# Seven query chunks in place of six in the first layer of a two-layer attention and gMLP kernel

## The chip, the cores and the metric

The kernel runs on one core of one Trainium2 chip. The metric is the device time of one execution in microseconds (us). A single execution of one kernel varies by up to 9 us in what follows, so times are medians of several runs, and the experiments below also use the clock that TensorE was granted in each run.

## The reference, cut to what matters

```python
def reference(A_x, A_wq, A_wk, A_wv, A_wo, B_x, B_w_in, B_w_sp, B_b_sp, B_w_out):
    x = A_x                                        # (1, 2048, 512), bf16
    x = x + _A_ref(_layernorm(x), ...)             # attention: 32 heads of 16, one K and V for all
    x = x + _B_ref(_layernorm(x), ...)             # gMLP: gelu, spatial 2048x2048 product, gate
    x = x + _A_ref(_layernorm(x), ...)             # the second layer, with the same weights
    x = x + _B_ref(_layernorm(x), ...)
    return x
```

The exps of the attention are the bulk: 2 layers x 32 heads x 2048 x 2048. The kernel works in blocks of 128 keys x 512 columns (queries times heads); there are 4096 of them.

## The kernel before

The kernel is a program that writes a program. It declares operations with dependences, an estimated duration and a priority. A greedy list scheduler inside it plays the five engines forward in time on those estimates, and at each step commits the operation that can start next. What it commits is written out as fixed instruction streams with semaphores. So the order of all instructions is settled before anything runs, and it depends on every estimate. `layer` is 0 for the first and 1 for the second layer; the lists below have one entry for each.

```python
self.chunks = [[512, 512, 512, 256, 128, 128]] * 2          # queries per chunk, for each layer
self.passes = [[(0, 8, 1), (8, 12, 2), (12, 15, 4)]] * 2    # spatial passes: key tiles s0:s1, after which chunk
self.gelus = [[(0, 1), (2,), (3, 4), (5,)]] * 2             # chunks whose GELUs are done together
...
def d_psum(n):                       # the estimates: VectorE on PSUM, ScalarE
    return n * 1.042e-3 + 0.066
def d_act(n):
    return n * 0.8333e-3 + 0.051
...
def make_q(self, q, war=()):         # the query projection of one set: n queries x 512/n slices of heads
    ...
    pairs = range(g.t0 // 256, (g.t0 + n - 1) // 256 + 1)
    pe_last, (op,) = sc.job([...], [...],
        [x for p in pairs for x in self.xnTA_ev[(g.layer, p)]] + self.c_wq[...], pr)
```

A query set of a chunk of 512 needs the transposed normalised X of four tiles (pairs 0 and 1); one of a chunk of 256 needs two tiles (pair 0). No score of a layer can be computed before its first query set is there. Each block of scores then gets its exp either on ScalarE (three or two blocks in one activation) or on VectorE (a chain of six instructions, two blocks at a time); the scheduler decides block by block. When a chunk's last group of heads is done, the chunk's output projection, layer norm and input product of the gMLP follow, among the exps of the next chunk. At the end of a layer comes the closing: the last spatial part, the gate, the output product, and, in the first layer, the keys of the second.

The softmax here doesn't subtract the row's maximum and nothing guards it: scores larger than these inputs give would overflow.

## Time and profile before

| | before |
|---|---|
| time, median of 3 runs | 1813.9 us (1811.8 to 1814.6) |
| span of the profiled run | 1813.8 us |
| ScalarE / VectorE busy | 96% / 95% |
| exp blocks on VectorE / on ScalarE | 532 / 3564 |

From the page of the kernel before. The first line is busy time, share of the span and number of instructions of each engine. The others are groups of instructions: line, engine, operation, tiles, shapes, count, then total busy us, mean ns of one, and the idle time before them.

```profile
PE 1579.3 (87%) x11647; PEld 463.8 (26%) x11730; DVE 1720.7 (95%) x2962; ACT 1732.7 (96%) x1561; POOL 48.5 (3%) x90
...
L1434 ACT ACTIVATE Pa<-ps_all 128x1024 bf16<-128x1024 f32 (+1 forms) x1430 | 1619.8, 1377 | 19.3 <-PE ps_all L1774 17.4
...
L1626 DVE TENSOR_SCALAR E<-ps_all 128x512 f32<-128x512 f32 x532 | 362.1, 684 | 23.3 <-PE ps_all L1774 20.5
L1755 PE MATMUL ps_all<-zero 128*128 128x512 bf16 x1066 | 326.8, 392 | 15.6 <-ACT z1s L1047 3.1
...
L1657 DVE SCALAR_TENSOR_TENSOR Pd<-E 128x1024 uint16<-128x1024 f32 x267 | 324.2, 1214 | 4.3
...
L1653 DVE TENSOR_TENSOR E<-E 128x1024 f16<-128x1024 f16 x267 | 182.7, 684 | 4.7
...
L1655 DVE TENSOR_TENSOR E<-E 128x1024 f16<-128x1024 f16 x267 | 182.3, 683 | 3.6
L1651 DVE TENSOR_SCALAR E<-E 128x1024 f16<-128x1024 uint16 x267 | 182.3, 683 | 1.6
...
L1654 DVE TENSOR_SCALAR E<-E 128x1024 f16<-128x1024 f16 x267 | 111.6, 418 | 2.1
```

TensorE (PE) has room: 327 us of its time are filler matmuls on a zero tile, which only keep it busy. ScalarE (ACT) and VectorE (DVE) are both full. The two are within a per cent of each other (96% and 95%).

The timeline of ScalarE of the kernel before: start us, us, engine, line, operation, tiles, shapes, count, and in brackets the idle time before it with what ended it.

```profile
9.24 0.98 ACT L725 ACTIVATE kT<-ps_all,mask 128x256 bf16<-128x256 f32 x2 [1.00 <-PE ps_all L703]
...
12.87 1.02 ACT L681 ACTIVATE xnTA<-ps_all 128x1024 bf16<-128x1024 bf16 x1 [0.93 <-PE ps_all L673]
...
14.21 0.59 ACT L828 ACTIVATE qs<-ps_all 128x512 bf16<-128x512 f32 x1
...
15.79 1.45 ACT L1434 ACTIVATE Pa<-ps_all 128x1536 bf16<-128x1536 f32 x1
```

The keys of pair 0 (kT) are copied by 10.2 us, but the queries (qs) only by 14.8 us, since they wait for pair 1; the first exp of the kernel starts at 15.79 us. ScalarE does not stand idle until then: between 12.87 and 15.79 us it does other copies (kT, V and xnTA, the transposed X), with one gap of 0.19 us. The next two lines are from the same engine's timeline at the boundary between the layers, where the exps of the first layer have ended (the table load follows the last one) and those of the second begin. The last line is from VectorE's timeline: the eviction of the first group of heads, a good mark of progress, as there are 64 of them.

```profile
864.86 1.28 ACT L1451 ACT_TABLE_LOAD   x1
...
900.72 1.45 ACT L1434 ACTIVATE Pa<-ps_all 128x1536 bf16<-128x1536 f32 x1 [1.25 <-PE ps_all L1774]
```

```profile
48.70 0.68 DVE L841 CAST oT<-ps_all 128x512 bf16<-128x512 f32 x1
```

### The profile page before, as it was taken

How to read it: one execution, taken by the hardware profiler on the slowest of the kernel's cores; microseconds unless marked ns; L12 is line 12 of the kernel's file. 1: busy time of each engine (PE TensorE's matmuls, PEld its weight loads, DVE VectorE, ACT ScalarE, POOL GpSimd, SP SyncE). 2: the span in 40 equal slices, each digit the busy share in tenths (PEclk: the TensorE clock that was granted, in tenths of full speed). 3: DMA queues.
4: the chain of work that ended last, by engine and by line, in shares of the span. 5: the costliest groups of instructions: out<-in, count | busy, mean ns of one | idle time of the engine just before them, and what ended most of it. 6: DMA issues, size and time to landing. Idle time of an engine off the chain costs nothing.

```text
span 1813.8 us, 29897 instructions
## 1 busy us (share of the span) xinstructions
PE 1579.3 (87%) x11647; PEld 463.8 (26%) x11730; DVE 1720.7 (95%) x2962; ACT 1732.7 (96%) x1561; POOL 48.5 (3%) x90
## 2 busy tenths in 40 slices
PE   8888888888889998898998888888888899989988
PEld 3222222222222222222432222222222222222334
DVE  8999999999999999987999999999999999999888
ACT  7999999999999999999589999999999999999983
POOL 2000000000000000000110000000000000000000
PEclk9999999999999999999999999999999999999999
DMA  5344110010010121121210001000110111212213
GB/s 158 100 113 103 35 27 7 7 30 18 16 47 28 29 53 47 36 59 57 52 44 7 7 7 19 18 7 4 30 24 13 44 30 30 47 28 52 65 57 113
DMA packets 154517, 75.65 MB, mean 42 GB/s; under 512 B 108548, under 2 KB 150792, under 8 KB 154376
## 3 DMA queue, kind: packets, MB, share of 16 engines
q1 hardware_dynamic: 152792, 73.56, 15.7%
q8 instruction: 94, 1.54, 0.4%
q14 instruction: 47, 0.39, 0.1%
q10 hardware_dynamic: 1584, 0.16, 0.1%
HBM read 30.97 MB, written 17.83 MB: 27 GB/s over the span
## 4 chain that ended last, share of the span: by engine, by line
ACT 43%; DVE 23%; issue 17%; PE 16%; DMA 1%; POOL 0%; ACTq 0%; POOLq 0%
ACT Pa L1434 41%; PE ps_all L1774 5%; DVE E L1626 3%; PE ps_all L1517 3%; PE ps_all L1158 3%; DVE Pd L1657 3%; DVE E L1653 2%; DVE st L641 2%; DVE E L1651 2%; DVE E L1655 2%; PE ps_all L1250 2%; PE ps_all L1755 1%; DVE gp L1171 1%; DVE E L1654 1%; DVE xn L656 1%
## 5 line engine op out<-in xcount | busy, mean ns | idle before, releaser
L1434 ACT ACTIVATE Pa<-ps_all 128x1024 bf16<-128x1024 f32 (+1 forms) x1430 | 1619.8, 1377 | 19.3 <-PE ps_all L1774 17.4
L1774 PE MATMUL ps_all<-qs,kT 32*128 32x512 bf16 x4096 | 566.5, 386 | 185.6 <-ACT Pa L1434 172.4
L1626 DVE TENSOR_SCALAR E<-ps_all 128x512 f32<-128x512 f32 x532 | 362.1, 684 | 23.3 <-PE ps_all L1774 20.5
L1755 PE MATMUL ps_all<-zero 128*128 128x512 bf16 x1066 | 326.8, 392 | 15.6 <-ACT z1s L1047 3.1
L1774 PEld LDWEIGHTS ps_all<-qs,kT 32*128 32x128 bf16 x4096 | 139.7, 91 | 766.4 <-ACT Pa L1434 725.8
L1657 DVE SCALAR_TENSOR_TENSOR Pd<-E 128x1024 uint16<-128x1024 f32 x267 | 324.2, 1214 | 4.3
L1517 PE MATMUL ps_all<-Pa,V 128*32 128x512 bf16 x3564 | 323.7, 387 | 1.6 <-DVE oT L841 1.6
L1158 PE MATMUL ps_all<-wsT,z2n 128*128 128x512 bf16 x674 | 192.8, 382 | 8.5 <-issue 3.8
L1653 DVE TENSOR_TENSOR E<-E 128x1024 f16<-128x1024 f16 x267 | 182.7, 684 | 4.7
L1517 PE MATMUL ps_all<-Pd,V 128*32 128x512 bf16 x532 | 186.1, 386 | 0.0
L1655 DVE TENSOR_TENSOR E<-E 128x1024 f16<-128x1024 f16 x267 | 182.3, 683 | 3.6
L1651 DVE TENSOR_SCALAR E<-E 128x1024 f16<-128x1024 uint16 x267 | 182.3, 683 | 1.6
L1755 PEld LDWEIGHTS ps_all<-zero 128*128 128x128 bf16 x1066 | 79.9, 98 | 182.1 <-issue 124.1
L1654 DVE TENSOR_SCALAR E<-E 128x1024 f16<-128x1024 f16 x267 | 111.6, 418 | 2.1
L1517 PEld LDWEIGHTS ps_all<-Pa,V 128*32 128x32 bf16 x3564 | 64.6, 94 | 123.2 <-issue 112.7
L1171 DVE TENSOR_TENSOR gp<-ps_all,gp 128x512 f16<-128x512 f32 x112 | 75.1, 686 | 19.0 <-PE ps_all L1158 19.0
L1158 PEld LDWEIGHTS ps_all<-wsT,z2n 128*128 128x128 bf16 x714 | 55.3, 98 | 92.0 <-issue 47.7
L980 PE MATMUL ps_all<-w_in_r,xnTB 128*128 128x448 bf16 x256 | 62.1, 355 | 2.2 <-DMA xnTB<-xn 0.7
L1016 PE MATMUL ps_all<-xnTB,w_in_r 128*128 128x512 bf16 (+2 forms) x336 | 62.5, 310 | 1.5 <-DVE z1s L1027 1.0
L1250 PE MATMUL ps_all<-E 128*128 128x512 bf16 x214 | 52.8, 380 | 4.9 <-DVE E L1235 4.0
L841 DVE CAST oT<-ps_all 128x512 bf16<-128x512 f32 x64 | 43.8, 684 | 1.3 <-PE ps_all L1517 1.2
L645 POOL TENSOR_SCALAR ve<-mv 128x2 f32<-128x2 f32 (+1 forms) x28 | 7.8, 277 | 1384.3 <-DVE mv L643 1384.1
(87 smaller groups left out, 915.4 us busy)
## 6 DMA issues: line engine op xcount, KB each, us to landing
wsT_scratch<-gp SPq DMA_DIRECT2D x16, 512.0 KB, 3.6
wsT<-wsT_scratch SPq DMA_DIRECT2D x8, 1024.0 KB, 5.4
z1s<-z_scratch SPq DMA_DIRECT2D x16, 448.0 KB, 3.7
wsT<-wsT_scratch SPq DMA_DIRECT2D x8, 512.0 KB, 3.8
z_scratch<-z1s SPq DMA_DIRECT2D x4, 896.0 KB, 5.7
X<-in_A_x_dram SPq DMA_DIRECT2D x8, 256.0 KB, 5.6
out_dram<-X SPq DMA_DIRECT2D x16, 128.0 KB, 2.1
w_in_r<-in_B_w_in_dram SPq DMA_DIRECT2D x1, 1792.0 KB, 10.2
```

The source lines that it names most:

```text
L1158: ins = e.matmul(self.b32(b), self.z2n[:, s, f * 128:(f + 1) * 128], w_[:, s - s0, :] if s - s0 < na or not spare else wsp[:, s - s0 - na, :],
L1171: return e.tensor_tensor(dst, self.b32(b), dst, ALU.add)
L1434: return e.activation(k.Pa[:, base:base + n, :], k.b32(b0, n).rearrange("p (k q) -> p k q", k=n), ACTF.Exp, scale=SCALE)
L1517: ins = e.matmul(k.b32(u.grp.pvb)[32 * j:32 * j + 32, :], k.V[:, u.kt, 32 * j:32 * j + 32], b.slot, tile_position=(0, 32 * j), start=u.fir ...
L1626: c = k.sc.op("dve", lambda e: e.tensor_scalar(k.ey[:, s, 512 * i:512 * (i + 1)], k.b32(j.bank.idx)[:, 0:512], E_LOG2, E_BIAS, op0=ALU.mul ...
L1651: o2 = sc.op("dve", lambda e: e.tensor_scalar(x, lo, E_X * 2.0 ** -16, E_X * E_A, op0=ALU.mult, op1=ALU.add), d_sb(n, 0.521e-3), self.ops ...
L1653: o3 = sc.op("dve", lambda e: e.tensor_tensor(w, x, x, ALU.mult), d_sb(n, 0.521e-3), [o2, self.wfree], pr)
L1654: o4 = sc.op("dve", lambda e: e.tensor_scalar(w, w, E_C, None, op0=ALU.add), d_sb(n, 0.26e-3), [o3], pr)
L1655: o5 = sc.op("dve", lambda e: e.tensor_tensor(w, w, x, ALU.mult), d_sb(n, 0.521e-3), [o4], pr)
L1657: o7 = sc.op("dve", lambda e: e.scalar_tensor_tensor(po.bitcast(U16), y, E_D, w, op0=ALU.add, op1=ALU.add), d_sb(n, 1.042e-3), [o5] + self ...
L1755: return e.matmul(k.b32(pvb if b is None else b.idx), k.zero[:], k.zero[:, None, :].to_broadcast([P, 4, P]), start=b is not None, stop=b i ...
L1774: return e.matmul(self.b32(bank), self.kT[32 * j:32 * j + 32, g.v, kt * 128:(kt + 1) * 128], self.qs[32 * j:32 * j + 32, g.q.slot, :], til ...
```

## The change

The first layer gets chunks 256, 256, 512, 512, 256, 128, 128. Its first query set then needs only the first pair of X tiles, so that the exps can begin earlier. The ends of chunks that the spatial passes hang on (1024, 1536 and 1920 queries) stay. The second layer stays as it was.

```diff
-        self.chunks = [[512, 512, 512, 256, 128, 128]] * 2
-        self.passes = [[(0, 8, 1), (8, 12, 2), (12, 15, 4)]] * 2
-        self.gelus = [[(0, 1), (2,), (3, 4), (5,)]] * 2
+        self.chunks = [[256, 256, 512, 512, 256, 128, 128], [512, 512, 512, 256, 128, 128]]
+        self.passes = [[(0, 8, 2), (8, 12, 3), (12, 15, 5)], [(0, 8, 1), (8, 12, 2), (12, 15, 4)]]
+        self.gelus = [[(0, 1, 2), (3,), (4, 5), (6,)], [(0, 1), (2,), (3, 4), (5,)]]
```

## The prediction

> **What bounds the kernel now.** The page's busy shares: ScalarE 96%, VectorE 95% of 1813.8 us; TensorE's 87% contains 1066 filler matmuls on the zero tile (327 us in the groups), so it has slack. The exp of the attention runs on both ScalarE and VectorE, and the kernel's scheduler shares it out, so in steady stages both are full: in 1000 to 1200 us ScalarE 100%, VectorE 97.6% (table of windows). So time is won only where one of them idles, and extra work on either costs about half its length, as the other takes over part of the exp.
>
> **Where they idle.** At the two layer ends. In the timeline of ScalarE layer 0's last exp ends at 864.9 and layer 1's first begins at 900.7. ScalarE is 45% busy from 866 to 893, 48% from 893 to 900.7, 79% from 900.7 to 940. VectorE is 97 to 100% busy from 880 on, with the closing of layer 0; that sets when each pair of key tiles is ready.
>
> **What the change moves.** The first query set of layer 1 now needs the normalised X of two tiles (one pair) and not of four. In the trace pair 0's transposes are copied by 890.3, its keys by about 892; pair 1's by 895.8, the query projection runs 896.8 to 898.8, the first scores start 900.3, the first exp 900.7. With one pair the projection can run about 891 to 892, the copy end about 893 and the first exp start at about 894 to 895: 6 us earlier. The ramp ran one activation of 1.45 us every 2.2 us, so about three fit into those 6 us: 4.3 us of ScalarE. But ScalarE did 3.1 us of copies for pair 1 there (transposes, keys, V, query), some of which moves to the full VectorE and delays the closing by about 1 us. Net, ScalarE's idle time falls by about 3 us, worth 1.5 us of time shared between two engines.
>
> **What it adds.** Chunk 0's eight groups of normalisations were one 256-wide instruction each (415 ns) and are now two of 128 (282 ns): +0.15 us x 8 = 1.2 us of VectorE. [...] here 2x282-415 = 149 ns shows it. The z1 evictions add 0.15 us, the GELUs (one of 3176 to two of 1682 ns) 0.2 us of ScalarE. Exp work, query sets (16), table loads, spatial passes and the end of layer 1 stay. Together +1.5 us of work, +0.8 us of time.
>
> **Sum.** 1813.9 - 1.5 + 0.8 = about 1813; with the earlier exp kept whole and a shorter ramp about 1810. The greedy schedule is rebuilt for all of layer 1, which may move it either way by some us. I say 1811.8, 8 in 10 between 1806 and 1817.5. Faster by over 2%: 0.01; within 2%: 0.98; slower: 0.01.
>
> **What would show it.** First exp of layer 1 at 894 to 895 instead of 900.7; ScalarE over 65% busy in 893 to 900.7; VectorE still full from 880 to 935; last key copy (about 939) no earlier, perhaps 1 us later; 16 narrower normalisations more; layer 1's closing unchanged, its last exp only 1 to 3 us earlier.
>
> **What would make it wrong.** The closing, short of banks or of ScalarE's help, is stretched by more than the early exps win; chunk 1's query projections, now in the first four sets, get in front of it; or the rebuilt schedule opens waits elsewhere.

## More of the kernel before

A block of exp costs ScalarE 1619.8 us / 3564 = 0.454 us. It costs VectorE 0.684 + (1.214 + 0.684 + 0.683 + 0.683 + 0.418) / 2 = 2.525 us.

## The result, and the profile after

| | before | after |
|---|---|---|
| time, median of 4 runs | 1813.3 us (1811.8 to 1814.6) | 1810.4 us (1809.1 to 1814.6) |
| ratio after / before | | 0.9988, 95% interval 0.9970 to 1.0007 |
| span of the profiled run, granted clock | 1813.8 us, 0.992 | 1807.8 us, 0.997 |
| exp blocks on VectorE | 532 | 528 |

A ratio is the mean time of one kernel's fast runs over that of the other's of the same rounds, so it is not quite the ratio of the medians. The time lies inside the predicted range, and the interval contains 1: from these runs alone it is not certain that anything was gained.

The lines of the page of the changed kernel that answer to those above:

```profile
PE 1572.3 (87%) x11677; PEld 467.0 (26%) x11764; DVE 1714.6 (95%) x2962; ACT 1731.6 (96%) x1557; POOL 50.4 (3%) x90
...
L1434 ACT ACTIVATE Pa<-ps_all 128x1024 bf16<-128x1024 f32 (+1 forms) x1430 | 1620.7, 1384 | 13.6 <-PE ps_all L1774 11.7
...
L1626 DVE TENSOR_SCALAR E<-ps_all 128x512 f32<-128x512 f32 x528 | 358.2, 681 | 23.9 <-PE ps_all L1774 21.0
```

ScalarE's busy time hardly moved (1732.7 to 1731.6 us). Of the 6 us by which this profiled span is shorter, 4.9 are idle time of ScalarE that is gone: 81.1 us before (1813.8 - 1732.7), 76.2 us after. The two profiles also differ in granted clock (0.992 and 0.997), and that alone is worth about 5 us by the slope found below, so they do not show by themselves what was gained. The profile of e1_again (the same changed kernel, clock 0.993) has 77.0 us of idle ScalarE in a span of 1809.7 us. The timeline of ScalarE in the changed kernel, at the start and, in the second fence, between the layers; in the third, the first eviction in VectorE's timeline:

```profile
9.34 0.98 ACT L725 ACTIVATE kT<-ps_all,mask 128x256 bf16<-128x256 f32 x2 [1.00 <-PE ps_all L703]
...
11.14 0.60 ACT L828 ACTIVATE qs<-ps_all 128x512 bf16<-128x512 f32 x1 [0.28 <-PE ps_all L818]
...
12.57 6.88 ACT L1434 ACTIVATE Pa<-ps_all 128x1536 bf16<-128x1536 f32 x6 [0.17 <-PE ps_all L1774]
```

```profile
859.76 1.28 ACT L1451 ACT_TABLE_LOAD   x1
...
894.71 1.45 ACT L1434 ACTIVATE Pa<-ps_all 128x1536 bf16<-128x1536 f32 x1 [0.94 <-PE ps_all L1774]
```

```profile
45.86 0.68 DVE L841 CAST oT<-ps_all 128x512 bf16<-128x512 f32 x1
```

The first exp of the whole kernel starts at 12.57 us and not at 15.79, 3.2 us earlier, because the queries are ready at 11.7 us. The first eviction comes 2.8 us earlier. Between the layers little changed: from the table load to the next exp it is 35.0 us, before it was 35.9. So the early exps of the change are at the start of the kernel, and the prediction had looked for them between the layers. It had taken the first entry of the list for the second layer's.

ScalarE did not gain 3.2 us of work by that, as part of the copies that it did there before went to VectorE. The same stretch in the two kernels, before and after; columns: stretch, its us, then busy us (and instructions) of PE, PEld, DVE, ACT and POOL, PEclk (the granted clock), DMA share, GB/s:

```profile
12.50:16.00 3.50, 3.50 (x47) 2.48 (x45) 3.50 (x11) 2.90 (x6) 1.71 (x4) 1.00 1.03 406
```

```profile
12.50:16.00 3.50, 2.79 (x33) 1.70 (x29) 3.50 (x11) 3.43 (x3) 0.90 (x3) 1.00 1.03 405
```

From 0 to 16 us ScalarE is busy for 7.49 us before and 8.62 us after. The early start takes 1.1 us of idle time from it by then, and not 3.2.

Of the evictions, the 8th comes 1.4 us earlier than before, the 16th 4.6, the 32nd (the last of the first layer) 4.8, and the 64th 6.45 us. The lead of 2.8 us is neither kept as it is nor lost. What else moves it is the question of the experiments.

### The profile page after: what moved, and what is told of

The parts are those of the page before. It is cut to its first block, busy times and chain, and to the rows that moved or that the text cites. A ratio compares the mean times of both kernels' runs of the same rounds, so it can differ in the third digit from the quotient of the medians.

```text
span 1807.8 us, 29941 instructions
## 1 busy us (share of the span) xinstructions
PE 1572.3 (87%) x11677; PEld 467.0 (26%) x11764; DVE 1714.6 (95%) x2962; ACT 1731.6 (96%) x1557; POOL 50.4 (3%) x90
## 4 chain that ended last, share of the span: by engine, by line
ACT 37%; DVE 27%; PE 19%; issue 16%; POOL 1%; DMA 1%; ACTq 0%; POOLq 0%
ACT Pa L1434 36%; PE ps_all L1774 5%; PE ps_all L1158 4%; DVE E L1626 4%; DVE Pd L1657 4%; PE ps_all L1517 3%; DVE E L1655 2%; DVE E L1653 2%; PE ps_all L1250 2%; DVE E L1651 2%; DVE st L641 2%; DVE gp L1171 1%; DVE E L1654 1%; PE ps_all L1755 1%; DVE z2n L991 1%
## 5 line engine op out<-in xcount | busy, mean ns | idle before, releaser
L1434 ACT ACTIVATE Pa<-ps_all 128x1024 bf16<-128x1024 f32 (+1 forms) x1430 | 1620.7, 1384 | 13.6 <-PE ps_all L1774 11.7
L1626 DVE TENSOR_SCALAR E<-ps_all 128x512 f32<-128x512 f32 x528 | 358.2, 681 | 23.9 <-PE ps_all L1774 21.0
```

What stands on the lines that cost most here:

```text
L1434: return e.activation(k.Pa[:, base:base + n, :], k.b32(b0, n).rearrange("p (k q) -> p k q", k=n), ACTF.Exp, scale=SCALE)
L1626: c = k.sc.op("dve", lambda e: e.tensor_scalar(k.ey[:, s, 512 * i:512 * (i + 1)], k.b32(j.bank.idx)[:, 0:512], E_LOG2, E_BIAS, op0=ALU.mul ...
```

## The experiments

Theory S (start): the change gains what the first exp comes earlier. Rivals: T, fewer stretches with a throttled TensorE clock; C, chance in the schedule, since the greedy scheduler orders the whole program anew after any change. All twelve kernels gave correct results, and each was timed in five rounds.

**Clock.** The clock records of the traces show TensorE at half speed in stretches of 3.4, 6.8 or 10.2 us. Counted in windows of 3.4 us, there are eight in the profile before (mean clock 0.992) and three in that after (0.997). Within one kernel the time follows the granted clock. Over the 99 timed runs with a listed clock, the deviations from each kernel's own mean in its job give 1.01 us for each 0.001 of clock. So the table also has each kernel's mean time brought to the clock 0.995 by this slope, with its standard error. The three jobs' runs of the kernel before then agree within 0.15 us (1813.13, 1813.25 and 1813.10). Differences below are worked out from unrounded means. This correction is an estimate; a kernel may also get a better clock by its own merit.

| run | first exp, us | ratio to before, 95% | mean clock | time at clock 0.995 | runs |
|---|---|---|---|---|---|
| before | 15.8 | | 0.9944 | 1813.2 +- 0.1 | 31 |
| changed (first job and e1_again) | 12.6 | 0.9988, 0.9994 | 0.9939 | 1811.2 +- 0.4 | 9 |
| e2_held_start | 15.6 | 1.0012 (0.9997 to 1.0027) | 0.9954 | 1816.8 +- 0.3 | 5 |
| e3_second_only | 15.9 | 1.0017 (1.0004 to 1.0029) | 0.9922 | 1814.6 +- 0.3 | 5 |
| e4_late_split | 15.8 | 1.0008 (0.9995 to 1.0020) | 0.9946 | 1815.4 +- 0.3 | 5 |
| e5_old_pa | 15.8 | 1.0012 (1.0000 to 1.0025) | 0.9952 | 1815.6 +- 0.3 | 5 |
| e6_new_pa | 12.4 | 0.9996 (0.9982 to 1.0009) | 0.9950 | 1812.4 +- 0.1 | 6 |
| e7_old_pb | 14.5 | 1.0036 (1.0024 to 1.0048) | 0.9930 | 1817.5 +- 0.2 | 6 |
| e8_new_pb | 12.9 | 1.0052 (1.0037 to 1.0067) | 0.9943 | 1822.0 +- 0.5 | 6 |
| e9_late_first_exp | 15.6 | 1.0009 (0.9996 to 1.0022) | 0.9936 | 1814.3 +- 0.3 | 5 |
| e10_same_start | 12.4 | 1.0022 (1.0010 to 1.0034) | 0.9942 | 1816.9 +- 0.4 | 5 |
| e11_old_best | 15.9 | 0.9997 (0.9984 to 1.0011) | 0.9937 | 1812.0 +- 0.4 | 6 |
| e12_both_best | 12.5 | 0.9965 (0.9953 to 0.9977) | 0.9970 | 1809.5 +- 0.3 | 5 |

### e1_again: the changed kernel once more

> The changed kernel once more, unedited, to have it on the same chip and in the same rounds as the next three. Both theories: 0.998 to 0.9995 of the kernel before (1 to 3.5 us less), first exp at 12.5 to 12.7 us. Its runs also list the granted clock: if throttling and not the early start makes the difference (rival), its time should follow the clock from run to run by more than the 2 to 3 us that the change is worth, and its clock should be higher than that of runs of other kernels with the old start.

Measured: median 1813.9 us, ratio 0.9994 (0.9982 to 1.0007), clock 0.991 to 0.995. The mean of its five runs is 2.2 us above that of the first job's four, at a clock 0.0024 lower; at clock 0.995 the two jobs give 1811.1 and 1811.4. So the change is worth 1.9 us at equal clock (standard error 0.4), and the clock of one run can hide that. The first sign of rival T came true: the five runs spread over 4.7 us, with the clock. But the clock is not what the change gains: over all runs it was no higher for the changed kernel (0.9939) than for the kernel before (0.9944). Rival T falls.

What a half-speed window costs can be read from two profiles of the same instruction stream, with the same columns as above. First the changed kernel of the first job, then e1_again:

```profile
501.70:505.10 3.40, 1.76 (x14) 0.43 (x13) 3.40 (x10) 3.39 (x3) 0.00 (x0) 1.00 0.70 206
505.10:508.50 3.40, 2.90 (x21) 0.73 (x21) 3.28 (x6) 3.40 (x5) 2.39 (x2) 1.00 0.99 332
```

```profile
501.70:505.10 3.40, 1.72 (x14) 0.39 (x13) 3.40 (x10) 3.39 (x3) 0.00 (x0) 1.00 0.71 209
505.10:508.50 3.40, 3.20 (x10) 0.62 (x10) 3.24 (x6) 3.02 (x4) 2.43 (x2) 0.50 0.98 330
```

Both executions do the same up to 505.1 us, with TensorE about half busy just before (1.76 and 1.72 of 3.40 us). In one the clock then goes to half (PEclk 0.50) for three windows, in the other it stays (1.00). What decides that was not found. By the 20th eviction e1_again is 2.0 us behind; at the 18th it was level. That is 0.7 us for a window. Another place of these profiles shows 0.5 us: at 716 to 720 us PEclk is 0.59 in e1_again and 1.00 in the other, and e1_again falls from 2.0 to 2.5 us behind between the 26th and the 28th eviction. Over the whole span the mean clocks are 0.997 (the three windows) and 0.993, which is about seven windows (estimated from that mean).

### e2_held_start: the changed kernel with the old start

```diff
-            [x for p in pairs for x in self.xnTA_ev[(g.layer, p)]] + ...
+            [x for p in (range(0, 2) if g.layer == 0 and g.ci == 0 else pairs) for x in self.xnTA_ev[(g.layer, p)]] + ...
```

> The changed kernel, with the query projections of chunk 0 of the first layer also waiting for the second pair of X tiles, as in the kernel before. Start theory (the gain is the first exp of the whole kernel coming 3.2 us earlier): first exp back at 15 to 16 us, the first group's eviction at 48 to 49 us and not 45.9, and 2.5 to 3.5 us slower than the changed kernel of the same rounds, so level with the kernel before or up to 1 us slower (ratio 0.9995 to 1.0008). Rival (a luckier schedule or fewer throttled windows): within 1 us of the changed kernel, ratio 0.9975 to 0.999.

Measured: the first exp is back at 15.60 us and the first eviction at 47.75 us, but the kernel is 5.6 us slower than the changed one at equal clock and 3.6 us slower than the kernel before. Theory S allowed 2.5 to 3.5 us. The start explains the first 1.9 us (47.75 - 45.86); the rest appears later. At the 8th eviction the held kernel is only 0.3 us behind the changed one, at the 12th 4.3 us. Its VectorE took 524 blocks and not 528, and was 94% busy. So the undone start is seen at the first evictions, and more is lost later than that; it is put down to the new order here, but was not traced. Neither theory's expected time came true. (The 48.70 us of the profile before contain a half-speed window at 21 us: PEclk is 0.60 from 21.0 to 22.9 us and 0.50 from 22.9 to 24.5. e4, which has the same old start, has 47.77 us. By the slope above, a window of 3.4 us at half speed costs about 0.95 us, an estimate that fits this difference of 0.93. The lead from the start itself is therefore put at 1.9 us at the first eviction, and not at 2.8.)

### e3_second_only: the change where the prediction had put it

The seven chunks stand in the second layer's entry and the six in the first's.

> The seven chunks in the second layer and the old six in the first: the place in which the prediction on record reckoned, by a misreading of which layer is changed. As it was reckoned there: the first exp of the second layer about 6 us earlier (gap from the last exp of the first layer 29 to 31 us and not 35.8), two to three exps more before the last key copy, and 1 to 3 us less than the kernel before (ratio 0.9983 to 0.9995). Rival: the closing of the first layer, which fills VectorE there, is stretched by what the early exps take from ScalarE's copies, and nothing is left (ratio 1.000, plus or minus 0.0005), although the first exp is early.

Measured: 1.5 us slower than the kernel before at equal clock, ratio 1.0017. The mechanism of the prediction is there, as ScalarE's timeline of e3 shows:

```profile
864.16 1.28 ACT L1451 ACT_TABLE_LOAD   x1
...
892.60 1.45 ACT L1434 ACTIVATE Pa<-ps_all 128x1536 bf16<-128x1536 f32 x1 [0.84 <-PE ps_all L1774]
```

The gap from the table load to the next exp is 28.4 us and not 35.9, so that exps start over 7 us earlier, and 21 instead of 17 activations of three blocks run while the keys are being made. But the keys are finished later. The last key copy on VectorE, first of e3 and then of the kernel before:

```profile
941.59 0.48 DVE L723 TENSOR_SCALAR kT<-ps_all,mask 128x256 bf16<-128x256 f32 x1
```

```profile
940.56 0.48 DVE L723 TENSOR_SCALAR kT<-ps_all,mask 128x256 bf16<-128x256 f32 x1
```

Counted from the table load, the last key copy comes 77.4 us after it and not 75.7. But 77.4 us is not long for this kernel: the changed kernel, without early exps at this place, takes 77.9 us (937.62 - 859.76), and the other versions that have the gap of some 34 to 36 us take 76.4 to 78.7. So the longer closing can't be put down to the early exps. At the 33rd, 34th and 35th eviction e3 leads by 1.3, 0.2 and 0.9 us, of which it had 0.7 before the closing. So the early exps came, and little or nothing of them was left by then. Neither of the two expected ratios came true. Where the exps were lost, and how much of the 1.5 us is chance of the order, this run does not separate.

### e4_late_split: the same split, not at the front

```diff
-        [256, 256, 512, 512, 256, 128, 128]
+        [512, 256, 256, 512, 256, 128, 128]
```

> First layer in chunks 512, 256, 256, 512, 256, 128, 128: the same two halves and the same added instructions, but not at the front, so no earlier start. Start theory: 0.3 to 1.5 us slower than the kernel before (added work 1.3 us of VectorE and 0.2 of ScalarE, shared by two engines), ratio 1.0002 to 1.0008, first exp at 15.8 us. Rival (seven chunks as such spread the work after each chunk better, or make a luckier schedule): as fast as the changed kernel, ratio 0.9975 to 0.9992.

Measured: first exp at 15.82 us, 2.3 us slower than the kernel before at equal clock. The rival (seven chunks as such are better) did not come true in this build. One build does not rule it out, as the scatter of e5 to e8 shows, and e12, the fastest version, has seven chunks in both layers. The cost is larger than the 0.3 to 1.5 us expected. By the exchange rate of the profile the added work (1.4 us of VectorE, 0.2 of ScalarE) should cost about 0.15 x 1.4 + 0.85 x 0.2 = 0.4 us, an estimate, so most of the 2.3 us is something else; the order is the candidate, which this run does not test.

### e5 to e8: reorderings without meaning

Both kernels, each with one of the scheduler's own estimates raised by 5 ns. What is computed stays the same; only the greedy scheduler's choices change: the order, and which engine does a block.

```diff
 # pa
-    return n * 0.8333e-3 + 0.051
+    return n * 0.8333e-3 + 0.056
 # pb
-    return n * 1.042e-3 + 0.066
+    return n * 1.042e-3 + 0.071
```

> Control of schedule chance: the kernel before, with the kernel's own estimate of a ScalarE instruction raised by 5 ns (0.051 to 0.056 us). Nothing is computed differently, but the greedy list schedule comes out in another order. Start theory: within 1 us of the kernel before at equal granted clock. Rival (schedule chance of the size of the change): 1.5 us or more away from it, to either side.

> The changed kernel with the same 5 ns. Start theory: 1.5 to 3 us less than e5 at equal granted clock, as the changed kernel is against the kernel before (1.9 us so far). Rival: the difference to e5 is of another size, below 0.5 or above 4 us, or of the other sign.

> A second reordering without meaning: the kernel before, with the kernel's own estimate of a VectorE instruction on PSUM raised by 5 ns (0.066 to 0.071 us). Start theory: within 1 us of the kernel before at equal granted clock; rival: 1.5 us or more away.

> The changed kernel with the same second reordering. Start theory: 1.5 to 3 us less than e7 at equal granted clock. Rival: the three differences (unperturbed, with the first and with the second reordering) scatter by more than 2 us around their mean; then the 1.9 us of the change can't be put down to the start alone.

Measured at equal clock: the kernel before goes from 1813.2 to 1815.6 (pa) and 1817.5 us (pb); the changed one from 1811.2 to 1812.4 and 1822.0 us. The three differences between changed and old are -1.9, -3.2 and +4.5 us. They scatter as rival C said they would. Of the expectations of S, the first of the four failed, the second was slightly exceeded, the other two failed. The early start is there in all three pairs: the first evictions of the changed kernels come at 45.86, 45.71 and 45.88 us, those of the old ones at 48.70, 49.41 and 47.65 us. What comes later decides. From the pages of e7_old_pb and e8_new_pb, in this order:

```profile
PE 1579.1 (87%) x11676; PEld 466.7 (26%) x11760; DVE 1716.3 (94%) x2951; ACT 1733.9 (95%) x1558; POOL 50.7 (3%) x90
...
L1626 DVE TENSOR_SCALAR E<-ps_all 128x512 f32<-128x512 f32 x528 | 358.8, 682 | 22.4 <-PE ps_all L1774 18.9
```

```profile
PE 1584.1 (87%) x11723; PEld 471.3 (26%) x11806; DVE 1706.5 (94%) x2942; ACT 1734.4 (95%) x1560; POOL 53.7 (3%) x90
...
L1626 DVE TENSOR_SCALAR E<-ps_all 128x512 f32<-128x512 f32 x523 | 355.3, 682 | 30.6 <-PE ps_all L1774 28.1
```

In e8 VectorE got five blocks fewer and stood idle 8 us longer before this instruction. By the price of a block ScalarE should have 2.3 us more to do for that, but its busy time grew by 0.5 us only (1733.9 to 1734.4), so the five blocks do not explain the loss. In these two profiles e8 leads by 3.8 us at the 16th eviction and by 2.9 at the 24th, and is 2.6 us behind at the 32nd. So some 5.5 us are lost in the last eight groups of the first layer, where ScalarE is idle for 6.4 us in e8 against 1.8 us in e7 (the mean clocks of the two profiles are 0.996 and 0.995). Which wait makes that idle time was not traced further.

### e9_late_first_exp: the start alone, in a fixed order

One way to test the start without a new order is to leave the scheduler alone and edit its output: one idle copy of about 3.1 us in front of the first exp of the changed kernel.

```diff
+        self.idle = sb([P, 3500], mybir.dt.uint8, "idle")
+        x = [o for o in sc.commits if o.eng == "act" and o.table == "exp"][0]
+        first = x.fn
+
+        def hold(e):
+            e.activation(self.idle[:], self.wk_rep[:, 0, 0:1].to_broadcast([P, 3500]), ACTF.Copy)
+            return first(e)
+        x.fn = hold
         progs = emit_program(nc, self.es, sc)
```

> The changed kernel with its order of instructions kept to the last one, and one idle ScalarE copy of about 3.1 us put in front of the very first exp, so that this starts at about 15.6 us, as in the kernel before. Start theory (what the first exp comes earlier is kept to the end when the order stays): 1.5 to 3.1 us slower than the changed kernel at equal granted clock (1811.3 at 0.995), so 1812.8 to 1814.4, and every group's eviction that much later than in the changed kernel. Rival (the start is absorbed by slack later, and the change's gain is schedule chance alone): within 0.7 us of the changed kernel.

The timelines of ScalarE and, in the second fence, of VectorE in e9 (its lines are numbered eight higher):

```profile
12.59 3.12 ACT L549 ACTIVATE idle<-wk_rep 128x3500 uint8<-128x3500 bf16 x1 [0.17 <-PE ps_all L1782]
15.61 2.35 ACT L1442 ACTIVATE Pa<-ps_all 128x1536 bf16<-128x1536 f32 x2
```

```profile
49.62 0.68 DVE L849 CAST oT<-ps_all 128x512 bf16<-128x512 f32 x1
```

Measured: 1814.3 us at equal clock, 3.0 us slower than the changed kernel, for a first exp that came 3.0 us later. In the profile the first eviction is 3.76 us late, and so are the 2nd, the 4th, the 8th and the 18th, to 0.01 us. (The 0.7 us above the delay of 3.0 fit the half speed at 16.5 to 23.3 us, PEclk 0.50, which follows the pause; that it is the cause was not shown.) After that the two profiles part further, to 7.4 us at the 64th eviction, with a mean clock of 0.993 in e9 and of 0.997 in the changed kernel; the 3.0 us is the difference of means at equal clock. So theory S holds for its part: with the order fixed, a microsecond that ScalarE stands still before its first exp is a microsecond at the end. But e9 is not the changed order with the old start. The kernel before did useful copies while its exps waited; e9 does nothing then, and VectorE too comes to a stop after it (2.44 and 0.99 us of idle time, at 15.6 and 22.3 us). Without the idle copy ScalarE has done 5.5 us of work by 16 us, against 7.5 in the kernel before and 8.6 in the changed one. So 3.0 us is more than the early start can be shown to give, and the 1.1 us by which e9 is slower than the kernel before (standard error 0.3) is not the cost of the new order.

### e10_same_start: the same start, another order of chunks

```diff
-        [256, 256, 512, 512, 256, 128, 128]
+        [256, 512, 256, 512, 256, 128, 128]
```

> First layer in chunks 256, 512, 256, 512, 256, 128, 128: the same early start with the first 256 queries and the same number of chunks, in another order. If the start alone decided: first exp at 12.6 us, first eviction at 45.9 us and the time of the changed kernel, 1811.3 plus or minus 1 at clock 0.995. Rival (start lead of 1.9 us plus a schedule chance of some us either way): lead of 1.9 us at the first eviction, but a final time anywhere between 1809 and 1818; the kernel's own scheduler reckons it 3.3 us longer than the changed kernel, which would be 1814.6.

Measured: first exp at 12.40 us, first eviction at 46.95 us, and 1816.9 us at equal clock, 5.7 us slower than the changed kernel and 3.8 us slower than the kernel before. The early start is there and the gain is not. The start alone does not decide; rival C was right about the final time, though the first eviction led by 0.8 us and not by 1.9 (47.77 - 46.95).

### e11_old_best and e12_both_best: picking the order on purpose

The kernel's own scheduler ends with a reckoned length. It is no measurement, and the numbers of this paragraph are such reckonings, except where it says measured. Over 121 reorderings with the two estimates shifted by at most 0.5 ns, the old chunks give 1802.5 us on average (standard deviation 2.6), the changed ones 1800.7 (2.4). Both kernels as given lie over 3 us below their averages, at 1799.0 and 1797.4: they were, it seems, picked from many. The two averages differ by 1.8 us, so in the scheduler's own reckoning the change is worth that much over many orders; the three measured pairs (-1.9, -3.2 and +4.5 us) scatter far more. The two runs take the shortest of the 121 for the old chunks, and for seven chunks in both layers.

```diff
 # e11, old chunks
-    return n * 0.8333e-3 + 0.051
+    return n * 0.8333e-3 + 0.0507
 # e12, seven chunks in both layers
-    return n * 0.8333e-3 + 0.051
+    return n * 0.8333e-3 + 0.0505
-    return n * 1.042e-3 + 0.066
+    return n * 1.042e-3 + 0.0659
```

> The kernel before, its own estimate of a ScalarE instruction lowered by 0.3 ns (0.0510 to 0.0507 us): of 121 such meaningless reorderings the one that the kernel's own scheduler reckons shortest, 2.0 us below the kernel before. If schedule chance is as large as the change: 1810.5 to 1812.5 at clock 0.995, so level with the changed kernel, with the old start (first exp at 15.8 us). If the gain can only come from the start: 1813.2 plus or minus 0.7, as the kernel before.

> Seven chunks in both layers, with the ScalarE estimate lowered by 0.5 and the VectorE one by 0.1 ns: of the 121 reorderings the one that the kernel's own scheduler reckons shortest, 4.6 us below the changed kernel and 6.2 below the kernel before. If the scheduler's reckoning can be used to pick a lucky order: 1805.5 to 1809 at clock 0.995 (ratio to the kernel before 0.995 to 0.998). If it can't: 1811 to 1815, no better than the changed kernel.

Measured: e11, with the old start at 15.93 us, 1812.0 +- 0.4 us at equal clock, 1.1 us below the kernel before and within error of the changed one. Its ratio (0.9997) does not show that without the clock correction. e12: 1809.5 us at equal clock, slightly above the range expected for it but below both kernels. Its ratio to the kernel before is 0.9965 (0.9953 to 0.9977), inside the range expected, and the one version here that is clearly faster. Part of that ratio is its clock (0.9970), the highest of all; at equal clock it gains 3.7 us on the kernel before and 1.8 on the changed one. From its page:

```profile
PE 1583.2 (88%) x11807; PEld 471.2 (26%) x11807; DVE 1721.1 (95%) x2985; ACT 1728.1 (96%) x1550; POOL 54.5 (3%) x90
```

ScalarE has the least work of all kernels here (1728.1 us), and VectorE is as busy as in the kernel before.

## Why the prediction was right or wrong

The number was right: 1811.8 us predicted, 1810.4 us measured, within the range, and "within 2%" with it. Most of the argument behind the number was not, so that the number was right by luck: the range of 11.5 us also holds 1813.3, the kernel before.

- **What bounds the kernel**: right as far as the shares show. Both engines are full before and after. That the gain is idle time of ScalarE that went (81.1 to 76.2 us in the profiles) is not shown: e4 has 77.1 us in its profile (mean clock 0.997) and is slower than the kernel before at equal clock, and e12, the fastest, has 79.0.
- **"The first query set of layer 1 now needs the normalised X of two tiles", and the costing at the boundary between the layers**: this step failed. The first entry of the list is the first layer, so the earlier exp is at 12.6 us of the kernel. Where the prediction had put it, e3 measured a loss of 1.5 us and not a gain, with the chance of a new order in it: the exps came 7 us earlier there, but at the 34th eviction the lead was 0.2 us.
- **Two of the named signs came true all the same.** The first exp of the second layer was to come at 894 to 895 us; it came at 894.71. ScalarE was to be over 65% busy from 893 to 900.7 us. The same stretch before and after:

```profile
893.00:900.70 7.70, 6.87 (x48) 3.39 (x48) 7.53 (x23) 3.72 (x8) 1.09 (x4) 1.00 0.28 76
```

```profile
893.00:900.70 7.70, 6.87 (x47) 2.90 (x45) 7.59 (x20) 5.60 (x7) 0.94 (x2) 1.00 0.35 95
```

  ScalarE went from 3.72 to 5.60 us, 73%. Yet the gap between the layers had not changed; everything before it was some 5 us earlier. A sign given as an absolute time cannot tell an early start from a shift. The gap could (35.9 and 35.0 us), and it said no. Other signs failed: VectorE was 94% busy from 880 to 935 us and not full (51.5 of 55 us), the last key copy came 2.9 us earlier (937.62 and not 940.56), and the last exp 6.5 us earlier and not 1 to 3 (it ends at 1754.96 and not 1761.42).
- **"Extra work on either costs about half its length"**: not borne out. By the prices of a block, 0.454 and 2.525 us, a microsecond of ScalarE is worth 2.525 / (2.525 + 0.454) = 0.85 us when the scheduler may rebalance, and one of VectorE 0.15 us (estimates). With the order fixed, so that nothing moves to the other engine, e9 measured 3.0 us for 3.0. So 3 us less of idle ScalarE should be worth 2.5 to 3 us, and not the 1.5 of the prediction; how well the scheduler rebalances was not measured by itself.
- **What it adds**: the instructions were counted right. There are 16 more normalisations of 128 columns (32 for 16) and 8 fewer of 256. Splitting one cost 149 ns by the durations of the profile before (2 x 282 - 415) and 148 ns by those of the profile after (2 x 281 - 414). The cost was put at 0.8 us; e4, which has the split without the start, measured 2.3 us, with the chance of a new order in it.
- **"The greedy schedule is rebuilt for all of layer 1, which may move it either way by some us"**: right, except that the order of the whole program is rebuilt and not of one layer, and the largest term of all. Changes of 0.3 to 5 ns in two estimates moved the old kernel by -1.1, +2.5 and +4.3 us, and two of them moved the changed one by +1.1 and +10.7 us.

So the right total came from a wrong place, by luck. What the runs show for the 1.9 us gained at equal clock: the first exp comes 3.2 us earlier, ScalarE is idle for 1.1 us less by 16 us, the first eviction leads by 1.9 us against the same old start in e4 (45.86 and 47.77 us), and a pause put at that place comes out in full at the end (e9). How the 1.9 us divides between this start, the added work (0.4 us by the estimate above) and the chance of the order stays open, because no edit of the chunks leaves the order alone: with the early start other orders lose everything (e8, e10), and with the old start a lucky one gains 1.1 us (e11).

## What to carry to other kernels

When a greedy scheduler fixes the order, a change of 0.1% can't be judged from one build: reorder both versions without meaning a few times and compare the scatter, and to test one mechanism edit the scheduler's output and not its input. Price a microsecond of each engine by the exchange rate of the work they share, here 0.85 and 0.15 by estimate, before adding up gains and costs. A pause put into a fixed order tests what a delay costs, not what an earlier start gains: look also at what the engine did in the meantime. Write the signs of a mechanism as gaps or differences, not as absolute times, and look at which entry of a list the change is in.
